# A new order of the opening: sequence tables, fold of x and its small copies on VectorE, width and row-768 tables and the W casts on GpSimd

## The chip, the cores and the metric

One core of one Trainium2 chip. The metric is device time in microseconds (us) of one execution, median of several. Engines are named as in the profile: PE is TensorE, PEld its weight loads, DVE is VectorE, ACT is ScalarE, POOL is GpSimd, SP issues DMAs.

## The reference, cut to what matters

```python
X = fft(x, axis=1); X = fft(X, axis=2); x = X.real        # x: (8, 3072, 256)
h = maximum(x @ w_in, 0)                                  # w_in: (256, 1024)
u, v = h[..., :512], h[..., 512:]
v_n = (v - mean(v)) / sqrt(var(v) + 1e-6)                 # over the last axis
v_s = einsum('ts,bsd->btd', w_spatial, v_n) + b_spatial   # w_spatial: (3072, 3072)
out = (u * v_s) @ w_out
```

## The kernel before

The large product with `w_spatial` (W) is done in bf16 on PE. W comes as fp32 and untransposed, so in batch 0 it is prepared in 96 pieces: POOL casts a piece, PE transposes it, ACT or DVE copies it out of PSUM.

```python
def turn_w(wt, act=False):
    ...
    nc.gpsimd.tensor_copy(out=wb, in_=wr)          # the cast; 3 buffers wb, 6 buffers wr
    load_w()                                       # starts the load of a later piece
    for kk in range(GK):
        nc.tensor.transpose(pt[:, kk, :], wb[:, 128 * kk:128 * kk + 128], ident)
    ... copy pt to wt on DVE or ACT ...
```

The transform over the sequence is a cosine/sine product on PE. DVE first folds x by symmetry, three folds a batch, each with an even and an odd half. In each fold stand two tiny copies and a memset on POOL:

```python
def fold_even(plus, rev):
    sm = fpool.tile([P, 4, D], FP32, name="sm", tag="sm")
    nc.vector.tensor_tensor(out=sm, in0=plus, in1=rev, op=ALU.add)
    e = fpool.tile([P, 4, 129], FP32, name="e", tag="e")
    nc.gpsimd.tensor_copy(out=view(e, 0, [[129, 4], [128, 2]]), in_=...)   # 8 columns
    nc.vector.tensor_tensor(out=e[:, :, 1:128], ...)
    ...
def fold_odd(plus, rev, od, oe):                  # oe: POOL for one fold of batch 0, else DVE
    ...
    nc.gpsimd.memset(o[:, :, 0:1], 0.0)
    ...
    nc.gpsimd.tensor_copy(out=view(ho, 0, ...), in_=...)                   # 2 columns
```

Ahead of the folds come the tables: sequence tables (DVE, ACT), width tables with their product (DVE, ACT, PE), and tables for the rows 0, 768, 1536 and 2304 (`specials`). The width tables use a scratch that shares its buffer with `sm`:

```python
scd = fpool.tile([P, 3, P], FP32, name="scd", tag="sm")   # fpool has one buffer a tag
```

The v tiles make `v_n`, 128 rows each (`pv`, `r`, `v_t`); of batch 0's 24, seven stand ahead of the main loop. A tile of that loop is 24 matmuls of W with `v_n` (`pw`) and one tile of `u` (`pu`, made into `ut` by ACT). In the main loop of 24 tiles a batch, the folds of the next batch stand between the steps of this one; after every fourth tile DVE gates four PSUM results, that is, adds the bias and multiplies by `ut` (`tm`, `gt`).

Of the kernel before, what the change touches and what calls it, by code (L numbers as in the profile page):

```python
# [9 lines left out]
FP32 = mybir.dt.float32  # L10
BF16 = mybir.dt.bfloat16
I32 = mybir.dt.int32
AF = mybir.ActivationFunctionType
ALU = mybir.AluOpType
# [3 lines left out]
P = 128  # L18
# [3 lines left out]
DH = 512  # L22
B = 8
NA = 3
# [9 lines left out]
PI2 = 6.283185  # L34
MAGIC = 12582912.0


def view(t, off, dims):
    return bass.AP(t.tensor, t.offset + off, [list(t.ap[0])] + [list(d) for d in dims])
# [3 lines left out]
def kernel(  # L43
# [9 lines left out]
    nc = tc.nc  # L53
# [3 lines left out]
    const = ctx.enter_context(tc.tile_pool(name="const", bufs=1))  # L57
# [6 lines left out]
    fpool = ctx.enter_context(tc.tile_pool(name="fpool", bufs=1))  # L64
# [13 lines left out]
    spb = const.tile([P, 2, 4 * B], FP32)  # L78
    sgn = const.tile([P, 1], FP32)
    weo = const.tile([P, 2, DFF], BF16)  # L80
# [116 lines left out]
    idf = fpool.tile([P, P], FP32, name="idf", tag="eofold")  # L197
# [9 lines left out]
    for kk in range(2):  # L207
# [9 lines left out]
                   allow_small_or_imprecise_dtypes=True)  # L217
    nc.gpsimd.memset(sgn, -1.0)
# [37 lines left out]
    nc.vector.tensor_scalar(out=ksc[:, 0:2], in0=ksc[:, 0:2], scalar1=1.0 / 256.0,  # L256
                            scalar2=None, op0=ALU.mult)
    for kk in range(2):
        sc = ksc[:, kk:kk + 1]
        nc.vector.tensor_scalar(out=dt_, in0=dio, scalar1=sc, scalar2=MAGIC,  # L260
                                op0=ALU.mult, op1=ALU.add)
        nc.vector.tensor_scalar(out=dy, in0=dio, scalar1=sc, scalar2=None, op0=ALU.mult)
        nc.vector.scalar_tensor_tensor(out=dt_, in0=dt_, scalar=MAGIC, in1=dy,
                                       op0=ALU.subtract, op1=ALU.subtract)
        nc.vector.tensor_scalar(out=dy.bitcast(I32), in0=dt_.bitcast(I32),
                                scalar1=0x7FFFFFFF, scalar2=None, op0=ALU.bitwise_and)
        nc.scalar.activation(out=c2[:, kk, 0, :], in_=dy, func=AF.Sin, scale=-PI2,
                             bias=halfpi)
        nc.scalar.activation(out=c2[:, kk, 1, :], in_=dt_, func=AF.Sin, scale=PI2)
        nc.scalar.activation(out=c2[:, kk, 2, :], in_=dt_, func=AF.Sin, scale=-PI2)  # L270

    alt = spool.tile([P, 4], FP32, name="alt", tag="alt")
    nc.vector.tensor_scalar(out=alt[:, 0:1], in0=ksc[:, 0:1], scalar1=128.0,
                            scalar2=MAGIC, op0=ALU.mult, op1=ALU.add)
    nc.vector.tensor_scalar(out=alt[:, 1:2], in0=ksc[:, 0:1], scalar1=128.0,
                            scalar2=None, op0=ALU.mult)
    nc.vector.scalar_tensor_tensor(out=alt[:, 2:3], in0=alt[:, 0:1], scalar=MAGIC,
                                   in1=alt[:, 1:2], op0=ALU.subtract, op1=ALU.subtract)
    nc.vector.tensor_scalar(out=alt[:, 3:4].bitcast(I32), in0=alt[:, 2:3].bitcast(I32),
                            scalar1=0x7FFFFFFF, scalar2=None, op0=ALU.bitwise_and)  # L280
    for kk in range(2):
        for v in (1, 2):
            nc.vector.tensor_scalar(out=c2[:, kk, v, 0:1], in0=alt[:, 3:4],
                                    scalar1=-4.0, scalar2=1.0, op0=ALU.mult, op1=ALU.add)
    for v in range(3):
        for ch in range(2):
            pw_ = psM.tile([P, DH], FP32, name="pw_", tag="psM")
            for kk in range(2):
                nc.tensor.matmul(pw_, lhsT=c2[:, kk, v, :],
                                 rhs=winb[:, kk, DH * ch:DH * ch + DH],  # L290
                                 start=(kk == 0), stop=(kk == 1))
            dst = weo[:, v, DH * ch:DH * ch + DH] if v < 2 else wom[:, DH * ch:DH * ch + DH]
            nc.scalar.copy(out=dst, in_=pw_)
# [4 lines left out]
    def fold_even(plus, rev):  # L298

        sm = fpool.tile([P, 4, D], FP32, name="sm", tag="sm")  # L300
        nc.vector.tensor_tensor(out=sm, in0=plus, in1=rev, op=ALU.add)  # L301
        e = fpool.tile([P, 4, 129], FP32, name="e", tag="e")
        nc.gpsimd.tensor_copy(out=view(e, 0, [[129, 4], [128, 2]]),  # L303
                              in_=view(sm, 0, [[D, 4], [128, 2]]))
        nc.vector.tensor_tensor(out=e[:, :, 1:128], in0=sm[:, :, 1:128],  # L305
                                in1=view(sm, 255, [[D, 4], [-1, 127]]), op=ALU.add)
        evf = fpool.tile([P, 2, 129], FP32, name="evf", tag="evf")
        od = gxpool.tile([P, 2, 129], BF16, name="od", tag="od")
        ev = gxpool.tile([P, 2, 129], BF16, name="ev", tag="ev")
        nc.vector.tensor_tensor(out=od, in0=e[:, 0:2], in1=e[:, 2:4], op=ALU.subtract)  # L310
        nc.vector.tensor_tensor(out=evf, in0=e[:, 0:2], in1=e[:, 2:4], op=ALU.add)
        nc.vector.tensor_tensor(out=ev[:, 0], in0=evf[:, 0], in1=evf[:, 1], op=ALU.add)
        nc.vector.tensor_tensor(out=ev[:, 1], in0=evf[:, 0], in1=evf[:, 1],
                                op=ALU.subtract)
        return od, ev

    def fold_odd(plus, rev, od, oe):


        df = plus  # L320
        oe.tensor_tensor(out=df, in0=df, in1=rev, op=ALU.subtract)  # L321
        o = fpool.tile([P, 4, P], FP32, name="o", tag="o")
        nc.gpsimd.memset(o[:, :, 0:1], 0.0)
        oe.tensor_tensor(out=o[:, :, 1:128], in0=df[:, :, 1:128],  # L324
                         in1=view(df, 255, [[df.ap[1][0], 4], [-1, 127]]),
                         op=ALU.subtract)
        ovf = fpool.tile([P, 2, P], FP32, name="ovf", tag="ovf")
        ho = gxpool.tile([P, 2, P], BF16, name="ho", tag="ho")
        he = gxpool.tile([P, 2, P], BF16, name="he", tag="he")
        oe.tensor_tensor(out=ho, in0=view(o, 0, [[3 * P, 2], [1, P]]),  # L330
                         in1=view(o, 2 * P, [[-P, 2], [1, P]]), op=ALU.subtract)
        oe.tensor_tensor(out=ovf, in0=o[:, 0:2], in1=o[:, 2:4], op=ALU.add)
        oe.tensor_tensor(out=he[:, 0], in0=ovf[:, 0], in1=ovf[:, 1], op=ALU.add)
        oe.tensor_tensor(out=he[:, 1], in0=ovf[:, 0], in1=ovf[:, 1], op=ALU.subtract)
        nc.gpsimd.tensor_copy(out=view(ho, 0, [[P, 2], [1, 1]]),
                              in_=view(od, 129 + 128, [[-129, 2], [1, 1]]))
        return ho, he

    def specials():
# [12 lines left out]
        nc.vector.tensor_scalar(out=q, in0=q, scalar1=-1.5, scalar2=0.25, op0=ALU.add,  # L352
                                op1=ALU.mult)
        nc.vector.tensor_tensor(out=q, in0=q, in1=q, op=ALU.mult)
        nc.vector.tensor_scalar(out=q, in0=q, scalar1=0.25, scalar2=None, op0=ALU.is_lt)
        nc.vector.tensor_scalar(out=y, in0=y, scalar1=nsc[0:nb, 5:6], scalar2=0.25,
                                op0=ALU.mult, op1=ALU.mult)
        nc.vector.tensor_scalar(out=t, in0=y, scalar1=MAGIC, scalar2=None, op0=ALU.add)
        nc.vector.scalar_tensor_tensor(out=f, in0=t, scalar=MAGIC, in1=y,
                                       op0=ALU.subtract, op1=ALU.subtract)  # L360
        nc.vector.tensor_scalar(out=y.bitcast(I32), in0=f.bitcast(I32),
                                scalar1=0x7FFFFFFF, scalar2=None, op0=ALU.bitwise_and)
        nc.scalar.activation(out=sp4[:, 4, :], in_=y, func=AF.Sin, scale=-PI2,
                             bias=halfpi[0:nb])
        nc.scalar.activation(out=sp4[:, 5, :], in_=f, func=AF.Sin, scale=-PI2)
        sc = gxpool.tile([nb, 2, nb], BF16, name="sc", tag="sc", bufs=1)
        for i in range(2):
            nc.vector.tensor_tensor(out=sc[:, i, :], in0=sp4[:, 4 + i, :], in1=q,
                                    op=ALU.mult)
        nc.vector.tensor_scalar(out=view(sc, nb + 1, [[4, B]]), in0=view(sc, nb + 1, [[4, B]]),  # L370
# [6 lines left out]
                         stop=True)  # L377
        nc.vector.tensor_copy(out=spb, in_=pb[:, 0:2, :])
# [142 lines left out]
    def prep(b):  # L521
# [9 lines left out]
        def s_odd(a):  # L531
            od, ev = st_["ev"]
            ho, he = fold_odd(*st_["xt"], od, nc.gpsimd if b == 0 and a == 1 else nc.vector)
            st_["gx"].append((od, ev, ho, he))
# [53 lines left out]
    def piece(act=False):  # L588
        if todo:
            t = todo.pop(0)  # L590
            if t == len(wts):
                new_wt()
            turn_w(wts[t], act)

    specials()
    for i in range(12):
        for part in steps[i]:
            for f in part:
                f()
        if i in (3, 6, 8, 9, 10, 11):  # L600
            piece(i < 8)
        if i == 7:
            xrs[1] = turn_x(1)
    for i in range(7):
        for f in vs0[i]:
            f()
        piece()
# [80 lines left out]
```

## Time and profile before

| | before |
|---|---|
| median | 1487.32 us (1486.56 to 1491.51) |
| profiled run | 1485.39 us, span 1483.6, clock 0.980 |
| PE busy | 1365.6 us, 92% |
| PE idle 57 to 130 / 130 to 190 us | 19.2 / 17.8 us |
| PE waits for a gate after 200 us | 19.5 us, six times |

The prediction below shows the lines that carry this. The last row of the table: in the view of waits after 200 us, this is PE's only large wait (columns: engine and line, what it waited for, us in total, times, longest).

```profile
PE pw L487 <- DVE tm L492: 19.5, 6, 3.5
```

### The profile page before, as it was taken

Reading aid. Unit: us, or ns where it says so; the run is one execution under the profiler, and the core shown is the slowest. Engines: PE = TensorE matmul, PEld = TensorE weight load, DVE = VectorE, ACT = ScalarE, POOL = GpSimd, SP = SyncE. Lnnn points to the kernel's source line nnn. Section 1 sums busy time; section 2 is a strip of 40 time slices with the busy share of each in tenths; the row PEclk is TensorE's granted clock in tenths of the full one; section 3 lists DMA queues with packets and bytes.
Section 4 is the critical chain, followed back from the end, with each engine's and each line's share of the span. In section 5 each row is a group of like instructions: output and inputs, shape, how many; then the busy total and the mean of one; then the engine's idle time right before and its main releaser. Section 6 shows DMA issues by size and latency. Waiting matters only on the chain.

```text
span 1483.6 us, 17934 instructions
## 1 busy us (share of the span) xinstructions
PE 1365.6 (92%) x6935; PEld 672.4 (45%) x7071; DVE 732.9 (49%) x1468; ACT 461.5 (31%) x775; POOL 132.7 (9%) x230
## 2 busy tenths in 40 slices
PE   1476699999999999999999999999999999999998
PEld 0233355544444444444444444444444444444444
DVE  6666635655345633564345643565255553561212
ACT  4353234531244213431244212441234213431111
POOL 3542233301000000001000000000000000000000
PEclk9988999999999999999999999999999999999999
DMA  7493888746443463336443473335434443434441
GB/s 256 165 363 94 296 308 289 241 170 217 165 132 129 150 247 128 127 123 226 170 146 132 149 248 120 131 123 203 157 121 135 171 149 129 130 139 157 142 157 50
DMA packets 100598, 255.28 MB, mean 172 GB/s; under 512 B 13568, under 2 KB 60192, under 8 KB 100384
## 3 DMA queue, kind: packets, MB, share of 16 engines
q1 hardware_dynamic: 61440, 196.66, 38.9%
q10 hardware_dynamic: 29568, 44.05, 8.1%
q0 software_dynamic: 9504, 13.42, 2.8%
q8 instruction: 55, 0.90, 0.2%
q14 instruction: 31, 0.25, 0.0%
HBM read 210.80 MB, written 56.62 MB: 180 GB/s over the span
## 4 chain that ended last, share of the span: by engine, by line
PE 80%; DVE 7%; issue 5%; POOL 1%; DMA 1%; ACT 0%; POOLq 0%; DVEq 0%; ACTq 0%
PE pw L487 59%; PE po L503 6%; PE pu L479 5%; PE pv L445 5%; DVE tm L492 2%; DVE gt L495 2%; PE pe L399 1%; PE pt L149 1%; DMA wr<-in_moe_w_spatial_dram 1%; POOL wb L144 1%; DVE stt L449 1%; DVE sm L301 0%; DVE xt L321 0%; DVE o L324 0%; DVE e L305 0%
## 5 line engine op out<-in xcount | busy, mean ns | idle before, releaser
L487 PE MATMUL pw<-wt,v_t 128*128 128x512 bf16 x4500 | 1074.0, 382 | 37.5 <-DVE tm L492 19.5
L487 PEld LDWEIGHTS <-v_t 128*128 128x128 bf16 x4608 | 451.8, 98 | 576.5 <-issue 39.3
L492 DVE TENSOR_TENSOR tm<-pw,bbc 128x512 f32<-128x512 f32 x192 | 130.9, 682 | 264.5 <-PE pw L487 264.5
L449 DVE BATCH_NORM_STATS2 stt<-r 128x6 f32<-128x512 f32 x192 | 132.6, 690 | 160.9 <-ACT r L448 160.8
L481 ACT ACTIVATE ut<-pu 128x512 bf16<-128x512 f32 x192 | 114.6, 597 | 311.3 <-PE pu L479 223.7
L507 ACT COPY ot<-po 128x512 f32<-128x512 f32 x96 | 56.2, 585 | 311.2 <-PE po L503 310.7
L495 DVE TENSOR_TENSOR gt<-tm,ut 128x512 bf16<-128x512 f32 x192 | 136.0, 709 | 13.5
L448 ACT ACTIVATE r<-pv 128x512 f32<-128x512 f32 x192 | 110.8, 586 | 98.8 <-PE pv L445 89.2
L463 ACT ACTIVATE v_t<-r,rs 128x512 bf16<-128x512 f32 x96 | 78.1, 814 | 104.6 <-DVE rs L461 102.1
L503 PE MATMUL po<-wob,gt 128*128 128x256 bf16 x768 | 103.7, 280 | 1.7 <-DVE gt L495 1.4
L445 PE MATMUL pv<-weo,eo_t 128*128 128x512 bf16 x283 | 94.2, 386 | 5.2 <-ACT r L448 3.6
L479 PE MATMUL pu<-eo_t,weo 128*128 128x512 bf16 x278 | 93.5, 388 | 0.7
L503 PEld LDWEIGHTS <-gt 128*128 128x128 bf16 x768 | 76.8, 101 | 32.4 <-issue 3.3
L149 PE MATMUL pt<-ident,wb 128*128 128x128 bf16 x576 | 50.2, 229 | 41.7 <-POOL wb L141 26.7
L303 POOL COPY e<-sm 128x8 f32<-128x8 f32 x24 | 4.6, 193 | 847.0 <-DVE sm L301 839.8
L149 PEld LDWEIGHTS <-wb 128*128 128x128 bf16 x576 | 41.8, 103 | 66.4 <-POOL wb L141 28.5
L154 ACT COPY wt<-pt 128x768 bf16<-128x768 bf16 x49 | 38.9, 794 | 94.6 <-PE pt L149 94.5
L460 DVE RECIPROCAL rs<-rs 128x2 f32<-128x2 f32 x96 | 15.5, 161 | 88.5 <-ACT rs L456 88.5
L445 PEld LDWEIGHTS <-eo_t 128*128 128x128 bf16 x384 | 36.9, 99 | 44.6 <-issue 6.3
L465 DVE TENSOR_SCALAR v_t<-r,mv,rs 128x512 bf16<-128x512 f32 x96 | 53.4, 556 | 0.0
L152 DVE COPY wt<-pt 128x768 bf16<-128x768 bf16 x47 | 25.7, 549 | 45.2 <-PE pt L149 41.2
L401 ACT ACTIVATE eo_t<-pe,spb 128x384 bf16<-128x384 f32 (+1 forms) x32 | 35.8, 1118 | 34.4 <-PE pe L399 33.9
(219 smaller groups left out, 703.5 us busy)
## 6 DMA issues: line engine op xcount, KB each, us to landing
wt<-wtd SPq DMA_DIRECT2D x168, 768.0 KB, 4.4
wr<-in_moe_w_spatial_dram SPq DMA_DIRECT2D x96, 384.0 KB, 5.3
out_dram<-ot ACTq DMA_DIRECT2D x96, 256.0 KB, 3.9
wtd<-wt ACTq DMA_DIRECT2D x24, 768.0 KB, 5.8
xr<-in_x_dram POOLq DMA_DIRECT2D x32, 384.0 KB, 10.4
xt<-in_x_dram SPq DMA_DIRECT2D x21, 512.0 KB, 3.9
xt<-xr SPq DMA_DIRECT2D x21, 512.0 KB, 5.3
x<-in_x_dram SPq DMA_DIRECT2D x1, 1536.0 KB, 6.6
```

Of the source, the lines that this page charges most:

```text
L149: nc.tensor.transpose(pt[:, kk, :], wb[:, 128 * kk:128 * kk + 128], ident)
L445: nc.tensor.matmul(pv, lhsT=l, rhs=w, start=(kt == 0), stop=(kt == 1))
L448: nc.scalar.activation(out=r, in_=pv, func=AF.Relu)
L449: nc.vector.bn_stats(out=stt[:, jj, :], in_=r)
L463: nc.scalar.activation(out=v[:, i - 1, :], in_=r2[0], func=AF.Identity, scale=rs[:, 0:1], bias=rs[:, 2:3])
L479: nc.tensor.matmul(pu, lhsT=w, rhs=r, start=(kt == 0), stop=(kt == 1))
L481: nc.scalar.activation(out=ut, in_=pu, func=AF.Relu)
L487: nc.tensor.matmul(pw, lhsT=v[:, k, 128 * dt:128 * dt + 128], rhs=wt[:, kk, :], start=(k == 0), stop=(k == KT - 1))
L492: nc.vector.tensor_tensor(out=tm, in0=pw, in1=bbc[:, TC * c:TC * c + TC], op=ALU.add)
L495: nc.vector.tensor_tensor(out=gt, in0=tm, in1=ut, op=ALU.mult)
L503: nc.tensor.matmul(po[:, i, :], lhsT=gts[dt][:, t0:t0 + 128], rhs=wob[:, dt, :], start=(dt == 0), stop=(dt == NDT - 1))
L507: nc.scalar.copy(out=ot, in_=po)
```

## The change

The intent: DVE makes the sequence tables and folds at once. POOL makes the width and row-768 tables in place of DVE, and casts W while DVE folds. The fold's small copies go from POOL to DVE, and the zero column is set once; the one odd half-fold of batch 0 that POOL made goes to DVE too. (The cosines of the tables that move are now made from the square of a sine.) The core of the diff, cut:

```diff
+    ef = const.tile([P, 4, 129], FP32)
+    of = const.tile([P, 4, P], FP32)
+    nc.gpsimd.memset(of[:, :, 0:1], 0.0)
...
-        nc.vector.tensor_scalar(out=dt_, in0=dio, scalar1=sc, scalar2=MAGIC, ...)
+        nc.gpsimd.tensor_scalar(out=dt_, in0=dio, scalar1=sc, scalar2=MAGIC, ...)
...      (width tables, alt, row-768 tables likewise)
-        nc.gpsimd.tensor_copy(out=view(e, 0, [[129, 4], [128, 2]]),
+        nc.vector.tensor_copy(out=view(e, 0, [[129, 4], [128, 2]]),
...
-        nc.gpsimd.memset(o[:, :, 0:1], 0.0)
-        nc.gpsimd.tensor_copy(out=view(ho, 0, [[P, 2], [1, 1]]),
+        nc.vector.tensor_copy(out=view(ho, 0, [[P, 2], [1, 1]]),
...
-    specials()
-    for i in range(12):
-        ... fold and transform steps; a piece at i in (3, 6, 8, 9, 10, 11)
+    pb = specials()
+    for i in range(3):
+        piece(True)
+    width()
+    for a in range(NA):
+        ... fold a
+        if a == 0:
+            specials_out(pb)
+        piece(True)
+        piece(True)
+    ... transform steps with a piece each; then v tiles, a piece at every second
```

## The prediction

> **What bounds the kernel now.** I read the page first: busy shares, then the forty slices.
>
> ```profile
> PE 1365.6 (92%) x6935; PEld 672.4 (45%) x7071; DVE 732.9 (49%) x1468; ACT 461.5 (31%) x775; POOL 132.7 (9%) x230
> ...
> PE   1476699999999999999999999999999999999998
> ```
>
> TensorE (PE) is the bound of the whole, but its first five slices of 37 us are not full: 1, 4, 7, 6, 6 tenths. All that this change can win lies there. So I next cut the span by stage, with the view of busy time by stretch (columns: stretch, length, then busy us and instruction count of PE, PEld, DVE, ACT, POOL, then granted clock, DMA share, GB/s).
>
> ```profile
> 0.00:57.00 57.00, 7.70 (x28) 3.19 (x29) 41.84 (x81) 16.46 (x23) 25.11 (x47) 1.00 0.51 173
> 57.00:130.00 73.00, 53.77 (x328) 27.41 (x332) 41.68 (x101) 43.42 (x71) 26.97 (x34) 0.89 0.77 285
> 130.00:190.00 60.00, 42.21 (x267) 22.62 (x270) 42.25 (x62) 12.14 (x17) 20.54 (x31) 0.91 0.66 228
> 190.00:1483.00 1293.00, 1261.93 (x6319) 619.19 (x6442) 607.15 (x1224) 389.48 (x665) 60.07 (x119) 0.99 0.48 163
> ```
>
> Four stages. Opening (to 57 us): DVE makes tables and folds x, PE has nothing to do. Start of the main loop (57 to 130): transform of batch 0, v tiles, first W pieces; PE idle for 19.2 us. W pieces beside the fold of batch 1 (130 to 190): PE idle for 17.8 us. The rest: PE is busy 97.6%, so anything gained earlier should arrive at the end nearly one for one.
>
> Then PE's waits over the first 200 us (columns: engine and line, what it waited for, us in total, times, longest).
>
> ```profile
> PE pt L149 <- POOL wb L141: 26.7, 4, 17.3
> PE pw__241 L289 <- ACT scr L267: 25.8, 2, 24.5
> PE pt L149 <- POOL wb L144: 13.1, 4, 5.7
> PE pw L487 <- ACT v_t L463: 12.1, 6, 3.3
> ```
>
> The W casts on POOL (wb) are named for 39.8 us: 22.3 us of it in the opening (17.3 and 4.9, where POOL and DVE are folding), and 17.4 us after 130 us (0.9, 3.8, 1.5, 2.9, 2.6 and 5.7, added up from the waits of each 20 us). A cast takes 0.8 us, so why is it late? POOL's own waits between 115 and 200 us say it:
>
> ```profile
> POOL e L303 <- DVE sm L301: 23.7, 2, 16.7
> POOL ho L335 <- DVE ho L330: 17.5, 3, 6.8
> ```
>
> Two tiny column copies of the fold stand in POOL's order ahead of the casts, and POOL stands behind DVE's fold to do them. They are blocked at the head of the queue; the casts behind them, though ready, do not run.
>
> Last, the opening in order of time, for what DVE and POOL do to each other when both work (start, duration, engine, line, operation):
>
> ```profile
> 34.93 0.69 DVE L305 TENSOR_TENSOR e<-sm 128x508 f32<-128x508 f32 x1 [0.29 <-POOL o L323]
> ...
> 41.62 2.34 POOL L321 TENSOR_TENSOR x<-x 128x1024 f32<-128x1024 f32 x1
> 41.70 2.81 DVE L305 TENSOR_TENSOR e<-sm 128x508 f32<-128x508 f32 x1 [0.36 <-POOL e L303]
> 43.90 0.11 POOL L323 MEMSET o<- 128x4 f32 x1
> 44.04 1.58 POOL L324 TENSOR_TENSOR o<-x 128x508 f32<-128x508 f32 x1
> 44.54 1.37 DVE L310 TENSOR_TENSOR od<-e 128x258 bf16<-128x258 f32 x1
> ```
>
> The same DVE instruction takes 0.69 us alone and 2.81 us here, where it ends 0.55 us after POOL's ends: it stood still for POOL's whole instruction. They take turns.
>
> **What the Trainium skill says.** "SBUF — State Buffer", section "Who interferes with whom": VectorE and GpSimd share one pair of ports under an exclusive lock; a VectorE instruction with two SBUF inputs, or in a two-port mode, excludes a GpSimd instruction that reads SBUF, and whichever comes second waits it out. This trace agrees (the lines above). "GPSIMD Engine Reference", section "4.1 Engine selection": two-input elementwise work is about twice slower on GpSimd. The trace agrees: 1024 elements, 2.34 us on POOL, 1.22 us on DVE. "TensorE: Matmul & The Clock Gate", part 1, "What's actually happening": an idle TensorE falls to half rate until it has been busy for some us. Here six transposes take 0.82 us after a long wait and 0.50 us otherwise, so a wait removed returns a little more than its length.
>
> **Part by part: the opening.** Before: tables end on DVE at 22.8 us; width and row-768 tables run on DVE and, with waits on ACT and PE, hold it to 33.4; folds run 33.4 to 56.4 (first 6.7 us, second 7.5, third 8.8, the last two lengthened by POOL); the transform begins at 56.7. The intent is a fold at 22.8, which alone would be 10.6 us.
>
> I expect it to start later. The fold's first result (sm) lies in the buffer that also holds the width tables' scratch (scd, same tag, one buffer); in the order of the changed kernel the first sm waits for ACT and POOL as well as for its loads. Width scratch is free only when POOL's second round is over, and ACT reaches its first width sine only after the last sequence cosine, at 21.7. From there: sine 0.3, square and scale on POOL 0.7 (I estimate 0.4 for 128 elements of two inputs, 0.25 of one, from 2.34 us for 1024), four POOL operations 1.2, sine 0.3, two more 0.7, and about 1 us of turns and semaphores: 26 us.
>
> Fold 1 is 6.7 us plus two copies of about 0.15, or 7.0, and takes turns with some 13 tiny POOL operations of 0.1 us: to 34.5. Then DVE meets the copy out of the row-768 product, whose tables POOL has half done by then (it advances one operation for each of DVE's): I estimate 4 us of standing still and 0.4 for the copies, to 39. Folds 2 and 3 are 14 us of DVE. Beside them POOL can cast up to 12 W pieces before the transform (9 transposed ahead of it, 3 more buffers); each takes the lock for about 0.7 us. Ten of them in the fold are 7 us. Sum: 39 + 14 + 7 = 60 us. So the transform starts near 60, about 3.5 us **later** than before. That is the term I trust least: 54 to 65.
>
> **Start of the loop.** In return, 9 pieces are done ahead of the transform instead of 2; the v tiles ahead of the loop carry 4 pieces instead of 7, the first loop tile 4 instead of 7. Six pieces leave a stretch in which ACT and DVE set the pace (each takes 0.80 us of ACT or 0.55 of DVE, and 0.34 of PE). The first loop tile took 18.2 us with 7 pieces and the second 14.7 with 4, so 3.5 us there, and about 1.5 in the v tiles: **minus 5 us**. The 12.1 us of waits for v_t remain; nothing in the change touches that chain.
>
> **W beside the fold of batch 1.** POOL's copies and memset leave for DVE, so the 17.4 us of waits for the casts lose their cause. Not all comes back: DVE is busy 42.3 of these 60 us, and without the waits the stretch would be 42.6 us, so DVE would be full. Some of the wait becomes PE waiting for DVE (turned pieces in PSUM, gates). I count 11 of 17.4, **minus 11 us**.
>
> **The rest.** In each later batch one gate stands behind the fold and PE waits 3.2 us, six times. The DVE copy saves the trip to POOL (0.36 us idle) and costs about 0.25: under 1 us in all, not counted.
>
> Sum: +3.5 - 5 - 11 = -12.5 us; 1487.3 - 12.5 = **1475 us**, 0.8% faster.
>
> **Rivals.** First, the fold really starts near 23 and the casts cost DVE little: the transform then begins at 45 to 48, and with the same later parts the gain is 25 us, about 1462. For it: x's mirror is issued at 13.3 and lands 7.8 us later, in time. Against: the shared buffer and the turns. Second, DVE becomes the bound in both stages, the casts being paid in the fold: transform at 65, only 5 us back after 130; the gain is 2 us, 1485. For it: DVE's 42 us of work in a 43 us stretch. Against: its busy time includes standing still, and the copies in PSUM can lag by several buffers. Third, DMA becomes the bound: loads of W run earlier. From 150 to 160 it moved 413 GB/s, full; over 130 to 200 it moved 17.4 MB, which in 56 us is 310 GB/s. Tight, not binding, and starting loads in the idle 30 to 50 us helps.
>
> **Range and chances.** The parts are uncertain by 5, 2 and 5 us: 1464 to 1485. Faster by over 2% means under 1458, which needs the first rival and all of the 17.4 us as well: 0.05. Slower by over 2% needs 30 us lost where only 60 us of opening are touched: 0.01.
>
> **What would show each step.** First sm at 26 rather than 23; lone DVE fold instructions stretched by a cast's length; DVE idle before the copy of pb for some 4 us; transform's first product near 60; no wait of PE for the casts left between 130 and 190, but some for DVE; PE's share after that unchanged. I am wrong if the fold starts at 23, if POOL casts few pieces during it, or if DVE keeps up fully beside the casts.

## The result, and the profile after

| | before | after |
|---|---|---|
| median | 1489.41 us (1486.56 to 1492.29, 4 runs) | 1469.74 us (1468.6 to 1472.87, 4 runs) |
| ratio | | 0.9871, 95% interval 0.9843 to 0.9899 |
| profiled run | 1485.39 us | 1472.87 us |

Ratios here are the mean time of one kernel's fast runs over that of the other's in the same rounds, so not quite the ratio of the medians. The kernel is 1.3% faster: 19.7 us by the medians. The two profiled runs are only 12.5 us apart: the profile of before fell on a run faster than all those in the table, that of after on its slowest of four. Positions below come from these two profiles.

Busy time by stretch, after, columns as in the prediction:

```profile
0.00:57.00 57.00, 10.03 (x72) 5.85 (x73) 42.80 (x60) 21.89 (x30) 44.58 (x79) 0.94 0.77 261
57.00:130.00 73.00, 54.40 (x286) 26.13 (x284) 41.30 (x100) 39.39 (x64) 18.29 (x23) 0.79 0.64 226
130.00:190.00 60.00, 51.21 (x344) 28.41 (x345) 46.81 (x77) 17.15 (x25) 22.66 (x24) 0.94 0.71 258
```

Only the third stage is clearly fuller on PE: 51.2 us of 60 against 42.2. The first has the same DVE time and much more of POOL; the second is as empty as before, and its granted clock is lower, 0.79 against 0.89. PE's waits of the first 200 us, after:

```profile
PE pb L379 <- POOL sc L374: 36.9, 1, 36.9
PE pw L496 <- ACT v_t L472: 14.2, 7, 3.3
PE pe L408 <- DVE ev L319: 6.9, 1, 6.9
PE pw L496 <- DVE tm L501: 4.2, 2, 3.7
...
PE pt L151 <- POOL wb L143: 1.7, 2, 1.3
PE pt L151 <- POOL wb L146: 1.3, 2, 0.7
```

The waits for casts fell from 39.8 us to 3.0. In the opening their place was taken by a wait for the fold (6.9 us, the transform wants the third fold's `ev`) behind one for the row-768 tables. The opening in order of time, after (start, duration, engine, line, operation):

```profile
26.49 1.23 DVE L308 TENSOR_TENSOR sm<-x 128x1024 f32<-128x1024 f32 x1 [3.38 <-POOL scr L271]
...
37.36 4.67 POOL L143 CAST wb<-wr 128x768 bf16<-128x768 f32 x6
...
37.79 0.22 DVE L387 COPY spb<-pb 128x64 f32<-128x64 f32 x1 [4.14 <-PE pb L382]
...
38.16 4.95 DVE L308 TENSOR_TENSOR sm<-x 128x1024 f32<-128x1024 f32 x1
...
56.81 0.50 PE L408 MATMUL pe<-ct,ev 128*128 128x385 bf16 x1 [6.88 <-DVE ev L319]
...
60.05 0.17 DVE L341 COPY ho<-od 128x2 bf16<-128x2 bf16 x1
```

DVE is through with its tables at 23.1 and stands still for 3.4 us, until POOL's last width operation frees the shared buffer. It folds once, stands still for 4.1 us before the copy of the row-768 product, and then begins a `sm` that takes 4.95 us instead of 1.22, while POOL runs six casts in one go. The third fold ends at 60.2 instead of 56.4.

Where the time comes from shows best in one landmark that each loop tile has: the start of its `ut` activation on ACT. The table gives its distance from the kernel before, in the profiled runs (minus is earlier). The experiments' columns are explained in the next section.

| loop tile (start before, us) | after | e1 | e2 | e3 | e4 | e5 | e6 | e8 |
|---|---|---|---|---|---|---|---|---|
| 0 (83.6) | +1.4 | +0.4 | +1.5 | +0.9 | -3.9 | +2.9 | -9.2 | -8.8 |
| 3 (127.7) | +3.3 | 0.0 | +3.2 | +2.8 | -2.5 | +4.7 | -6.5 | -6.9 |
| 9 (199.2) | -10.0 | -13.3 | +7.4 | -10.3 | -15.9 | -9.6 | -21.8 | -20.1 |
| 190 (1466.0) | -12.5 | -15.4 | +5.3 | -13.0 | -18.1 | -12.4 | -23.1 | -55.0 |

After: the opening costs 1.4 us, the first three loop tiles another 1.9, and tiles 3 to 8 bring 13.3 us. This is the stage in which W is cast beside the fold of batch 1.

### The profile page after: what moved, and what is told of

The parts are those of the page before. It is cut to its first block, busy times and chain, and to the rows that moved or that the text cites. A ratio compares the mean times of both kernels' runs of the same rounds, so it can differ in the third digit from the quotient of the medians.

```text
span 1471.1 us, 18005 instructions
## 1 busy us (share of the span) xinstructions
PE 1372.1 (93%) x7071; PEld 673.5 (46%) x7071; DVE 740.0 (50%) x1491; ACT 464.2 (32%) x779; POOL 133.7 (9%) x187
## 4 chain that ended last, share of the span: by engine, by line
PE 84%; DVE 7%; ACT 1%; issue 1%; ACTq 0%; DVEq 0%
PE pw L496 63%; PE po L512 6%; PE pu L488 5%; PE pv L454 5%; DVE tm L501 2%; PE pt L151 1%; PE pe L408 1%; DVE gt L504 1%; DVE sm L308 1%; DVE xt L328 1%; DVE stt L458 1%; DVE of L330 0%; DVE ef L312 0%; ACT v_t L472 0%; ACT r L457 0%
## 5 line engine op out<-in xcount | busy, mean ns | idle before, releaser
L156 ACT COPY wt<-pt 128x768 bf16<-128x768 bf16 x53 | 42.0, 800 | 61.4 <-PE pt L151 61.0
L146 POOL CAST wb<-wr 128x768 bf16<-128x768 f32 x48 | 42.6, 895 | 78.4 <-PE pt L151 46.9
L143 POOL CAST wb<-wr 128x768 bf16<-128x768 f32 x48 | 42.1, 887 | 70.3 <-PE pt L151 40.2
L410 ACT ACTIVATE eo_t<-pe,spb 128x384 bf16<-128x384 f32 (+1 forms) x32 | 35.8, 1117 | 37.8 <-PE pe L408 37.8
```

## The experiments

Theory A: all of the gain is the freeing of POOL's queue in the fold of batch 1, and the new opening is worth nothing. Theory B: the opening brings half or more of it. Below A there was a second question: what holds the opening back.

**e1: only the copies.** The kernel before, with the fold's copies off POOL and a fixed buffer for the zero column. The opening's order is the old one, and in the one fold of batch 0 whose odd half POOL makes, POOL keeps the `ho` copy (`oe`).

```diff
-        e = fpool.tile([P, 4, 129], FP32, name="e", tag="e")
-        nc.gpsimd.tensor_copy(out=view(e, 0, [[129, 4], [128, 2]]),
+        e = ef
+        nc.vector.tensor_copy(out=view(e, 0, [[129, 4], [128, 2]]),
-        o = fpool.tile([P, 4, P], FP32, name="o", tag="o")
-        nc.gpsimd.memset(o[:, :, 0:1], 0.0)
+        o = of
-        nc.gpsimd.tensor_copy(out=view(ho, 0, [[P, 2], [1, 1]]),
+        oe.tensor_copy(out=view(ho, 0, [[P, 2], [1, 1]]),
```

> The kernel before with one thing changed: the fold's two small copies and the memset leave POOL (DVE copies, one fixed buffer with its zero column set once). The opening order stays as before. Theory A (all the gain is the casts freed in the fold of batch 1; the new opening is worth nothing or costs 2 to 3 us): PE's waits for casts between 130 and 200 us fall from 17.4 to under 3 us, 10 to 14 us gained, ratio to before about 0.991, as good as the whole change or better. Theory B (the opening order brings half or more of the gain): 5 us or less, ratio 0.996 or above.

Measured: 1469.08 us, ratio 0.9867 (0.9850 to 0.9883), as good as the whole change. PE's waits from 130 to 200 us, e1, in full:

```profile
PE pw L489 <- DVE tm L494: 3.0, 3, 2.0
PE pt L151 <- DVE wt L154: 1.2, 1, 1.2
PE po__1732 L423 <- DVE he L335: 0.9, 1, 0.9
PE pw L489 <- issue: 0.2, 1, 0.2
```

No wait for a cast is left; 5 us of waits for DVE, busy 45.9 us of the 60, stand in their place. A few lines of the diff carry the whole gain; which of the three small operations matters most was not run.

**e2: only the opening.** The changed kernel, with copies and memset on POOL again from batch 1 on.

```diff
-            st_["ev"] = fold_even(*st_["xt"])
+            st_["ev"] = fold_even(*st_["xt"], nc.gpsimd if b > 0 else nc.vector)
-            ho, he = fold_odd(*st_["xt"], od)
+            ho, he = fold_odd(*st_["xt"], od, nc.gpsimd if b > 0 else nc.vector)
```

> The changed kernel with one thing undone: from batch 1 on the fold's copies and memset are on POOL again. The opening stays new. Theory A: the waits of PE for the casts come back, 12 to 18 us between 130 and 200, and the kernel is about as slow as before or 2 to 3 us slower, ratio 1.000 to 1.003. Theory B: at least half of the gain stays, ratio 0.994 or below.

Measured: 1490.92 us, ratio 1.0017 (1.0002 to 1.0032): all of the gain is gone, and the new opening by itself gains nothing. POOL's two large waits between 115 and 200 us come to the same totals in this run as in the kernel before:

```profile
POOL ef L311 <- DVE sm L309: 23.7, 2, 16.5
POOL ho L345 <- DVE ho L340: 17.5, 3, 6.8
```

PE waited 17.6 us for casts after 130 us, as before (17.4). e1 and e2 together settle theory A: with the copies alone the gain is there, without them it is not, whatever the opening.

**e3: scratch in its own buffer.** The changed kernel without the shared buffer.

```diff
-    scd = fpool.tile([P, 3, P], FP32, name="scd", tag="sm")
+    scd = fpool.tile([P, 3, P], FP32, name="scd", tag="scd")
```

> The changed kernel, but the scratch of the width tables has a buffer of its own instead of the one that the fold's first result needs. The first fold must then start at about 23 us instead of 26.5, if the shared buffer is what holds it. Theory A (DVE then meets the copy of the row-768 product, which POOL's chain of small operations sets): the first fold is over near 31, DVE stands still for 7 us instead of 4, the second fold starts at 38 or later as now, and the time is that of the changed kernel within 2 us. Theory B (the shared buffer is what costs the opening): the third fold ends 3 to 3.5 us earlier, and so does the kernel.

Measured: 1471.00 us, ratio 0.9890 (0.9875 to 0.9904). The first fold starts 3.5 us earlier and DVE then waits 2.8 us longer; DVE's lines, e3:

```profile
23.03 1.30 DVE L308 TENSOR_TENSOR sm<-x 128x1024 f32<-128x1024 f32 x1
...
37.30 0.22 DVE L387 COPY spb<-pb 128x64 f32<-128x64 f32 x1 [6.97 <-PE pb L382]
```

So the shared buffer did hold the fold, and freeing it alone is worth nothing: the next stop, the copy of `pb`, is set by POOL's chain of small operations and hardly moves (37.8 to 37.3).

**e4: few casts beside the folds.** The changed kernel with no piece ahead of the transform; POOL can cast only the three it has buffers for. Nine pieces go into the v tiles instead of four, three are left for the loop.

```diff
-    for i in range(3):
-        piece(True)
     width()
...
-        piece(True)
-        piece(True)
...
-        if i % 2 == 0:
-            piece()
+        piece()
+        if i < 2:
+            piece()
```

> The changed kernel with no W piece ahead of the transform: POOL can cast only the three for which it has buffers while DVE folds; 4 pieces go into the transform and 9 into the v tiles, 3 are left for the loop, as before. Theory A (each cast takes the lock from DVE for 0.7 us): the third fold ends near 54 instead of 60 us, and the first v tile comes 5 us earlier. If the v tiles are paced by their own chain of waits and not by the pieces, most of the 5 us stays: 3 to 5 us faster than the changed kernel. Theory B (the early pieces are worth their place): the pieces that now crowd the v tiles and the first loop tile take the 5 us back, same time or slower.

Measured: 1467.82 us, ratio 0.9869 (0.9855 to 0.9884); by the medians 1.9 us faster than the changed kernel, less than the 3 to 5 expected, and their ratios to before do not tell them apart. In the profiles the third fold ends at 54.5 instead of 60.2: 5.7 us, with nine casts fewer. Not all of it is the casts. In the changed kernel POOL also issues four loads of x beside the second fold, and DVE instructions that take 0.29, 0.29 and 0.17 us in the third fold take longer there, 1.7 us in all:

```profile
48.99 2.99 POOL L99 DMA_DIRECT2D xr<-in_x_dram  x4
...
49.68 0.79 DVE L339 TENSOR_TENSOR he<-ovf 128x128 bf16<-128x128 f32 x1
50.40 0.91 DVE L340 TENSOR_TENSOR he<-ovf 128x128 bf16<-128x128 f32 x1
51.23 0.79 DVE L341 COPY ho<-od 128x2 bf16<-128x2 bf16 x1
```

In e4 the same loads are issued from 37.3 to 40.3 and lengthen one DVE instruction by 0.5 us. That leaves about 4.5 us for the nine casts, 0.5 each.

From the first v tile to the first `ut` it takes 16.6 us with nine pieces (63.06 to 79.71), 15.7 with four in the changed kernel (69.27 to 84.98), 15.9 with seven before (67.73 to 83.63). Pieces do not pace the v tiles. A chain of waits of their own would fit; no run cuts that chain.

**e5: both stops of DVE removed.** e3, and the copy of `pb` after the third fold.

```diff
-        if a == 0:
+        if a == NA - 1:
             specials_out(pb)
```

> The changed kernel with both stops of DVE in the opening taken away: scratch of the width tables in its own buffer, and the copy of the row-768 product after the third fold instead of after the first. Theory A (two stops in a row, of which removing the first alone only lengthened the second): first fold at 23, no standing still of 4 or 7 us, third fold done at 50 to 54 instead of 60 us, and the first gate 6 to 8 us earlier; time near 1463. Theory B (POOL's work and the lock set the end whatever the order): POOL's small operations now wait for more of DVE's, the casts start later and run beside the third fold, which ends at 58 or later; within 2 us of the changed kernel.

Measured: 1470.97 us, ratio 0.9894 (0.9881 to 0.9908): a miss for theory A. The folds do run through, but the last but one operation falls on POOL's casts, e5:

```profile
43.76 4.97 DVE L340 TENSOR_TENSOR he<-ovf 128x128 bf16<-128x128 f32 x1
...
43.91 4.67 POOL L143 CAST wb<-wr 128x768 bf16<-128x768 f32 x6
```

An instruction that takes 0.28 us alone takes 4.97. And PE, which runs in order, has nine pieces and the width product ahead of the transform, all behind `pb`, which now comes at 43.3 instead of 36.9: its first transform product is at 54.9. The W loads start later with the casts, and PE waits another 3.4 us for a cast at 67.6. Theory B had the time right and the reason wrong: PE's order, not the end of the folds, now set the start.

**e6: e5 and e4 together.** No stops, no pieces in PE's way, and, as it came out, no cast beside the folds: POOL's first is at 46.9.

> The previous one and in addition no W piece ahead of the transform (three casts at most beside the folds). Theory A: third fold done at 48 to 50 us, first v tile 9 to 11 us earlier than in the changed kernel, and 7 to 10 us kept at the end; time near 1461. Theory B (later stage refills the gap): the pieces or the loads of W are then behind, PE waits for casts or for loads after 130 us; 3 us or less kept.

Measured: 1461.00 us, ratio 0.9828 (0.9814 to 0.9841), 8.7 us faster than the changed kernel. The folds end at 44.1, and the copy of `pb` waits 0.2 us, e6:

```profile
43.97 0.16 DVE L341 COPY ho<-od 128x2 bf16<-128x2 bf16 x1
44.35 0.22 DVE L387 COPY spb<-pb 128x64 f32<-128x64 f32 x1 [0.21 <-PE pb L382]
```

The first v tile comes at 57.8 instead of 69.3, 11.4 us earlier. This is the opening that the change intended: three things held it, in a row, and taking one (e3, e4) or two (e5) away showed little. The other two pairs were not run.

**e7: folds off the gate tiles.** The changed kernel with one number changed, for a wait that neither kernel touched.

```diff
-        df = 2 if b == 1 else 3
+        df = 2 if b else 3
```

> The changed kernel with one number changed: from batch 2 on the folds of the next batch stand in loop tiles 0, 2 and 4 instead of 0, 3 and 6, so that none stands in a tile whose PSUM results go through gates. It tests what the six waits of PE for a gate (3.2 us each) come from, which neither kernel touched. Theory A (the gate stands in DVE's order behind a fold): all six waits go, with the half-rate matmuls after each; 19 to 28 us gained, time 1443 to 1451. Theory B (something else paces the gate, or the x loads come too late for a fold two tiles on): PE waits the same, or for DVE in other tiles; 5 us or less.

Measured: 1438.95 us, ratio 0.9677 (0.9664 to 0.9691), 30.8 us faster than the changed kernel. First one of the six waits in the changed kernel, with the half-rate matmuls behind it (six take 1.46 us otherwise):

```profile
340.62 2.72 PE L496 MATMUL pw<-wt,v_t 128*128 128x512 bf16 x6 [3.20 <-DVE tm L501]
```

Then PE's waits after 200 us in e7, in full:

```profile
PE po L512 <- DVE gt L504: 1.4, 2, 1.1
PE pw L496 <- DVE tm L501: 0.2, 1, 0.2
```

The six waits came to 19.2 us and their removal returned 30.8, 5.1 us for each wait of 3.2. The rest is the half rate. In the changed kernel PE is busy throughout the 10 us after each wait, but at a granted clock of 0.70 to 0.87 (two of the six, columns as in the prediction):

```profile
340.62:350.62 10.00, 10.00 (x47) 4.94 (x47) 6.94 (x14) 1.18 (x2) 0.00 (x0) 0.84 0.77 281
508.45:518.45 10.00, 9.99 (x37) 4.56 (x37) 6.87 (x14) 1.18 (x2) 0.00 (x0) 0.70 0.74 274
```

10 us times what the clock lacks is 1.3 to 3.0 us a wait, 12.1 for the six, and 19.2 and 12.1 are 31.3. The gain exceeded my range because I had put the half-rate part at 0 to 1.5 us a wait.

**e8: e6 and e7 together.**

> The two before it together: no stops of DVE in the opening, few casts beside the folds, folds off the gate tiles. The stages are far apart, so the gains should add: 7 to 10 and 19 to 28 us off the changed kernel, time near 1438, ratio to the kernel before about 0.967. If they do not add, something shared (W loads, clock) takes part of it.

Measured: 1429.95 us (1427.40 to 1430.54), ratio 0.9614 (0.9601 to 0.9627): 3.9% faster than before, 39.8 us faster than the changed kernel. 8.7 and 30.8 are 39.5: they add.

## Why the prediction was right or wrong

The time was right, 1475 predicted with 1464 to 1485, 1469.74 measured, and so was "within 2%". By its own steps:

- **Opening, first stop.** Right: `sm` predicted at 26, found at 26.49, released by POOL's last width operation. e3 confirms the cause.
- **Opening, second stop.** Right: "4 us of standing still" before the copy, found 4.14; second fold predicted at 39, found at 38.2.
- **Folds beside the casts.** The sum was right: end near 60, found 60.2, but some of that is luck. Against the lengths of the same instructions alone, the twelve casts lengthened DVE's by 6.9 us, 0.6 each (0.7 foretold, for ten), and the loads of x, which I had not counted, by 1.7; in return the bare folds take 13.4 us and not 14, and began 0.8 us sooner. The picture of taking turns was too simple: six casts went by before DVE got its turn (4.95 us). The cost per cast is about the same either way.
- **Start of the transform.** I had it 3.5 us later, when the third fold is over. PE did not wait for all of it: two products ran at 49.4, the third at 56.8, when the even half of the third fold was done (before: the first at 56.7). The first v tile, behind the whole transform, came 1.5 us later.
- **Start of the loop, "minus 5 us".** Wrong, and the largest error. From the first v tile to loop tile 3 the changed kernel lost about 1.8 us (+1.5 to +3.3) instead of gaining 5. I took pieces to pace this stretch, from tile 0 with seven pieces (18.2 us) and tile 1 with four (14.7). But tile 0 with four pieces took 20.6 us in the changed kernel (80.83 to 101.41 on PE). So pieces do not set the pace: e4 with nine of them in the v tiles lost 0.9 us. That the v tiles' own chain sets it is my reading, not shown. The waits for `v_t` rose from 12.1 to 14.2 us, and the granted clock of this stage fell from 0.89 to 0.79. That clock goes with the pieces: between 57 and 130 us it is 0.78 to 0.82 in the kernels with nine pieces ahead of the transform (after, e2, e3, e5, e7) and 0.86 to 0.90 in those with two or none (before, e1, e4, e6). But it does not explain the loss, for from loop tile 0 to 3 e4 and e6 lose too, 1.4 and 2.6 us; the 1.8 us stay open.
- **W beside the fold of batch 1, "11 of 17.4".** The mechanism was right, shown by e1 and e2; the size was low: 13.3 us. DVE is busy 46.8 of 60 us there, and PE waits for it 5.7 us, so the lock and the fold did take a part back, as I had it, but a smaller one.
- **The rest, "not counted".** In the profiles another 2.5 us come in six small steps, one behind each gate wait: -1.4, +1.1, +0.1, -1.3, -0.9, -0.2. The waits are as long as before (19.2 against 19.5), but the half rate after them is not: over the 10 us after each the granted clock was 0.70 to 0.85 before and 0.70 to 0.87 after, which makes 13.7 us lost before and 12.1 after. With the waits that is 1.9 of the 2.5 us, and nothing in the change aims at it: which wait gets the longer stretch differs from run to run. The 7 us by which the medians differ more than the profiles stay open. The scatter of runs is of that size: e1's five run from 1464.89 to 1469.97.

So two errors of opposite sign met: 6.8 us too good at the start of the loop; 2.0 too bad before it, 2.3 beside the fold of batch 1 and 2.5 in the rest. The right sum hid them, by luck; only the landmarks by stage show it. And it is right for the pair of profiles (12.5 us); by the medians the gain was 19.7 where I had 12.3. Of the rivals, the first (fold at 23, all gained) needed three further edits (e6), the second (DVE as the bound after 130) was partly there, the third (DMA) did not show in PE's waits.

## What to carry to other kernels

A tiny instruction on a lightly used engine can cost most when it waits: what stands behind it in that engine's order waits as well, so look at the idle time before an instruction and at who needs the ones behind it. When an opening is held by several stops in a row, removing one can show nothing; take them away together before you call one harmless. And keep long runs of off-path work on an in-order engine away from the few instructions, like gates, that free another engine's buffers.

## What the Trainium skill lacked or had wrong

- "SBUF — State Buffer", section "Who interferes with whom", says that the second to issue waits until the first finishes. Here the waiting DVE instruction did not get the next turn: with six casts ready in POOL's queue it stood through the run of them, 4.95 us for 1.22 in the changed kernel and 4.97 for 0.28 in e5. In other places of the same trace they did take turns (two casts in 2.73 us around one DVE instruction); which of the two happens, no run here settles.
- "TensorE: Matmul & The Clock Gate", part 1, "What's actually happening", gives an idle window of about 3.4 us, running freely, before the rate is halved. Here shorter waits were followed by half rate: gate waits of 3.2 us (six matmuls in 2.72 us instead of 1.46), each worth 5.1 us when removed (e7), and one of 2.39 us at 80.03 in the changed kernel (two matmuls in 1.01 us instead of 0.59). A wait of 3.00 us in the kernel before, at 98.94, was not (two in 0.60). So the length of the wait alone does not decide; what does, no run here settles.
- No page that I used gives the time of short dependent operations in a chain on POOL. Here four 32-element operations in a row started 0.37 us apart in the changed kernel (34.32 to 35.43), against 0.20 to 0.26 on DVE in the kernel before; that chain set the second stop.
